# Pooled attention with an MLP: last keys scored over all rows, queries of two pairs transposed together, heads alternating in a batch's last pairs

## The chip, the cores and the metric

One core of a Trainium2 chip runs the whole program. The metric is device time in microseconds (us) of one execution. The kernel before takes 897.01 us, the median of three executions (896.06 to 898.55).

Engines as the profile names them: PE is the matrix engine, PEld its weight load, DVE the vector engine, ACT the scalar engine, POOL the GpSimd engine, SP the engine whose queue issues nearly all DMAs here.

## The reference

Four batches of eight heads, 1152 positions of 64 elements. Queries are averaged in twos, so 576 query rows stand against 1152 keys. The result, with the heads side by side (512 wide), goes through a layer norm and an MLP of width 2048 with a residual.

```python
def attn(q, k, v):                                    # (4, 8, 1152, 64) each
    q_pool = q.reshape(B, H, S // 2, 2, D).mean(axis=3)
    scores = np.matmul(q_pool, k.transpose(0, 1, 3, 2)) / np.sqrt(D)
    attn = np.exp(scores - np.max(scores, axis=-1, keepdims=True))
    attn = attn / (np.sum(attn, axis=-1, keepdims=True) + 1e-09)
    return np.matmul(attn, v)

x = attn_out.transpose(0, 2, 1, 3).reshape(B, S // 2, H * D)
xn = (x - mu) / np.sqrt(var + 1e-06) * g_ln
out = x + np.maximum(xn @ w_ch1, 0.0) @ w_ch2         # 512 -> 2048 -> 512
```

## The kernel before

**Tiling.** Heads are taken in pairs: 4 pairs a batch, 16 pairs in all, numbered p. A pair is nine steps, so there are 144 steps, numbered i with `p, j = divmod(i, 9)`. A step scores 128 query rows against all 1152 keys. Steps j = 0 to 3 are the first head, j = 4 is the last 64 rows of both heads, j = 5 to 8 the second head. Nearly every product is made with numbers split into a high and a low fp16 half, three matmuls for one (high by high, high by low, low by high).

**Scores** (`emit_s`, L320 to L344). The contraction is 64 long, and keys of even chunks lie on partitions 0 to 63, of odd chunks on 64 to 127. So the matmuls over 512 keys go in couples, one on the upper and one on the lower 64 rows of the array. The ninth chunk, the last 128 keys, has no partner: it takes three more matmuls of 128 columns on rows 0 to 63. A step has nine score matmuls (18 of half the width at j = 4).

**A step** (`step`, L924 to L986) is written out by hand. In program order a step i takes the row maximum of its scores (L350, DVE), issues the scores of step i + 1 (L337, PE), then for i the exponential (L364) and its high half (L378, both ACT). Then come the low half of step i - 1 (L387 on DVE; for j = 2, 5, 8 L244 and L385 on POOL), its DMA transpose through SP (L390), the product with V of step i - 4 (L433, 27 matmuls), one transposition for the next pair (`a_prep`) and one unit of the MLP (`some_units`). The first batch (steps 0 to 35, `on_pe`) is different: it transposes in fp32 on PE (L397, L421), has no MLP units, and DVE, ACT and POOL prepare the MLP's weights beside it.

**Next pair.** While a pair runs, k, v and q of the next come in through SP. The q tile holds two pairs, one on each half of the partitions, and has two buffers; its four loads stand together at step i0 - 2 of an even pair (i0 is the first step of the pair before it). POOL adds neighbouring queries (`pool_q`, L162) and copies the sum beside itself (`dup_q`, L168), ACT takes a bound of each tensor (`bound`, L180). Then `prep_k` and `prep_q` transpose on PE into a PSUM bank, and ACT and DVE split that into two fp16 halves. `PREPS` lists six for a pair: keys of each head, the last keys, and three units of six query chunks of 64 rows by 128.

**MLP units.** A 128-row tile t of a batch is normed (`norm`, `ln_a`, `ln_r`, `ln_t`) when all eight heads of it are there. Two normed tiles release `half_of` units into a queue: for each half w of the width four units of the first layer (L569, 24 matmuls) and four of the second (L600, 12 matmuls). The 64-row leftovers of two batches make a smaller set, `("h", g)`. A step takes one unit from the queue; after step 148 two. A batch of four tiles has 32 units. With the heads in order, tiles t = 0 to 3 of a batch become whole in the last pair's steps j = 5, 6, 7 and 8.

```python
key = ("h", b // 2) if j == 4 else (b, j if j < 4 else j - 5)
whole[key] = whole.get(key, 0) + 1
if whole[key] == 8 and key != ("h", 0):
    norms.append(key)
```

## Time and profile before

| what | value |
|---|---|
| median of three executions | 897.01 us |
| the profiled execution's own time | 892.43 us |
| its span from first to last instruction | 890.6 us |
| PE, DVE, ACT, POOL busy | 837.2, 611.8, 568.4, 346.6 us |
| granted PE clock, mean | 0.98 |

The busy time of PE is modelled from starts and sizes, and matmuls overlap in it, so a price is better read from the start of one group to the start of the next. The span runs from the first to the last instruction; the time of an execution is a little more.

### The profile page before, as it was taken

The numbers are of one execution on the slowest core, as the hardware profiler recorded it, in microseconds if no ns is written. First come the engines' busy times: TensorE is split into PE (matmuls) and PEld (weight loads), VectorE is DVE, ScalarE is ACT, GpSimd is POOL, SyncE is SP. The second block draws the span as 40 slices with busy tenths as digits, with TensorE's granted clock in tenths as the row PEclk, the third lists the DMA queues.
The fourth block names the chain that finished last, engine by engine and source line by source line (L and its number), as shares of the span: only waits on it lengthen the run. The fifth ranks groups of instructions, "written<-read, shape, count | busy, mean of one in ns | idle before, by whom it ended". The sixth has DMA issues, their size and how long they took to land.

```text
span 890.6 us, 22107 instructions
## 1 busy us (share of the span) xinstructions
PE 837.2 (94%) x9430; PEld 608.2 (68%) x9430; DVE 611.8 (69%) x1094; ACT 568.4 (64%) x851; POOL 346.6 (39%) x316
## 2 busy tenths in 40 slices
PE   8898979899799999996999999998999999999997
PEld 6787768677566676754758576676667576776664
DVE  3586988888787777778777777787777777532211
ACT  4888788788677777776677777676767666211110
POOL 3010543543988844336435243535543422300000
PEclk9999999999899999997999999999999999999999
DMA  4554154403498779997896979895979778310001
GB/s 130 196 157 164 50 194 126 172 1 96 92 179 168 141 150 183 180 169 137 154 193 114 203 141 188 127 186 107 222 121 175 129 129 143 57 25 13 13 13 24
DMA packets 271667, 114.95 MB, mean 129 GB/s; under 512 B 254928, under 2 KB 254928, under 8 KB 271568
## 3 DMA queue, kind: packets, MB, share of 16 engines
q1 hardware_dynamic: 271216, 112.65, 61.4%
q8 instruction: 74, 1.21, 0.6%
q10 hardware_dynamic: 352, 0.88, 0.4%
q14 instruction: 25, 0.20, 0.1%
HBM read 45.09 MB, written 4.72 MB: 56 GB/s over the span
## 4 chain that ended last, share of the span: by engine, by line
PE 54%; DVE 25%; ACT 10%; DMA 5%; issue 3%; POOL 2%; SPq 1%; ACTq 0%; POOLq 0%; DVEq 0%
PE psum L569 15%; PE psum L600 15%; DVE mx L350 7%; PE psum L337 7%; PE psum L433 7%; DVE hl L387 4%; PE psum L421 4%; DVE stage L107 3%; ACT pe L364 3%; PE psum L397 2%; DVE ht L583 2%; DVE wsl L107 2%; DVE kt L270 2%; DMA qr<-in_q_dram 2%; DMA kr<-in_k_dram 1%
## 5 line engine op out<-in xcount | busy, mean ns | idle before, releaser
L350 DVE TENSOR_REDUCE mx<-psum 128x1 f32<-128x1152 f32 x144 | 194.2, 1349 | 27.1 <-PE psum L433 18.9
L364 ACT ACTIVATE pe<-psum,nb,sc 128x1152 f32<-128x1152 f32 x144 | 188.9, 1312 | 32.0 <-DVE nb L355 23.6
L600 PE MATMUL psum<-wsl,ht 128*128 128x512 f16 x864 | 196.0, 379 | 0.2 <-DVE ht L583 0.2
L569 PEld LDWEIGHTS <-wsl 128*128 128x128 f16 x1920 | 170.9, 98 | 22.7 <-issue 2.7
L569 PE MATMUL psum<-xn,wsl 128*128 128x256 f16 x1536 | 177.3, 274 | 1.9 <-DVE xn L539 1.0
L337 PE MATMUL psum<-kt,qt 64*128 64x512 f16 (+3 forms) x1440 | 151.8, 332 | 24.7 <-ACT xb L488 13.9
L337 PEld LDWEIGHTS <-qt 64*128 64x128 f16 (+1 forms) x1440 | 70.9, 98 | 116.0 <-issue 66.4
L600 PEld LDWEIGHTS <-ht 128*128 128x128 f16 x864 | 81.8, 98 | 90.0 <-issue 0.4
L378 ACT ACTIVATE hl<-pe 128x1152 f16<-128x1152 f32 x108 | 125.7, 1163 | 5.0 <-DMA pt<-hl 1.6
L433 PE MATMUL psum<-vt,pt 128*128 128x65 f16 (+1 forms) x3240 | 119.8, 195 | 0.0
L433 PEld LDWEIGHTS <-pt 128*128 128x128 f16 (+1 forms) x3240 | 108.1, 101 | 9.4 <-issue 0.6
L488 ACT ACTIVATE xb<-psum,r 128x64 f32<-128x64 f32 x128 | 39.7, 311 | 109.4 <-DVE r L484 100.1
L244 POOL TENSOR_SCALAR pe<-pe 128x1152 f32<-128x1152 f32 x36 | 41.9, 1164 | 164.0 <-ACT hl L378 153.7
L387 DVE SCALAR_TENSOR_TENSOR hl<-pe,hl 128x1152 f16<-128x1152 f32 x72 | 104.3, 1448 | 0.0
L582 ACT ACTIVATE ht<-psum 128x512 f16<-128x512 f32 x72 | 42.7, 594 | 90.6 <-PE psum L569 90.2
L583 DVE SCALAR_TENSOR_TENSOR ht<-psum,ht 128x512 f16<-128x512 f32 x72 | 49.6, 690 | 66.2 <-ACT ht L582 65.4
L385 POOL TENSOR_TENSOR hl<-pe,hl 128x1152 f16<-128x1152 f32 x36 | 86.4, 2400 | 3.0
L421 PE MATMUL psum<-pt,vt 128*65 128x128 f32 (+1 forms) x720 | 81.6, 271 | 0.0
L421 PEld LDWEIGHTS psum<-pt,vt 128*65 128x65 f32 x720 | 75.8, 144 | 0.2 <-issue 0.2
L270 DVE SCALAR_TENSOR_TENSOR qt<-psum,s,qt 128x384 f16<-128x384 f32 x48 | 29.6, 616 | 46.9 <-ACT qt L273 46.9
L270 DVE SCALAR_TENSOR_TENSOR kt<-psum,s,kt 128x512 f16<-128x512 f32 (+1 forms) x48 | 31.5, 658 | 39.1 <-ACT kt L273 39.1
L403 ACT COPY pt<-psum 128x512 f32<-128x512 f32 x72 | 44.9, 639 | 10.8 <-PE psum L397 5.5
(112 smaller groups left out, 925.6 us busy)
## 6 DMA issues: line engine op xcount, KB each, us to landing
stage<-in_moe_w_ch_dram SPq DMA_DIRECT2D x32, 512.0 KB, 5.5
kr<-in_k_dram SPq DMA_DIRECT2D x16, 576.0 KB, 4.7
qr<-in_q_dram SPq DMA_DIRECT2D x31, 288.0 KB, 6.2
vr<-in_v_dram SPq DMA_DIRECT2D x15, 576.0 KB, 4.9
out_dram<-xb SPq DMA_DIRECT2D x32, 128.0 KB, 2.4
pt<-hl SPq DMA_TRANSPOSE x108, 5.0
vr<-in_v_dram ACTq DMA_DIRECT2D x1, 576.0 KB, 6.5
out_dram<-xh SPq DMA_DIRECT2D x4, 128.0 KB, 3.5
```

What stands on the lines that cost most here:

```text
L270: nc.vector.scalar_tensor_tensor(lo, ps, s, hi, op0=ALU.mult, op1=ALU.subtract)
L337: nc.tensor.matmul(out=sp[o:o + w, c0:c0 + n], lhsT=qt[r:r + 64, qa, q0:q0 + w], rhs=kt[r:r + 64, ka, h, k0:k0 + n], start=(a == 0), stop= ...
L350: nc.vector.tensor_reduce(mx, st["s"], axis=AX.X, op=ALU.max)
L364: nc.scalar.activation(out=st["pe"], in_=st["s"], func=ACTF.Exp, scale=pair[i // C]["sc"][:, 0:1], bias=st["nb"],)
L378: nc.scalar.activation(out=hl[:, 0], in_=st["pe"], func=ACTF.Copy, scale=2.0 ** 15)
L385: nc.gpsimd.tensor_tensor(hl[:, 1], st["pe"], hl[:, 0], op=ALU.subtract)
L387: nc.vector.scalar_tensor_tensor(hl[:, 1], st["pe"], 2.0 ** 15, hl[:, 0], op0=ALU.mult, op1=ALU.subtract)
L421: nc.tensor.matmul(out=ps[0:65, q0:q0 + w], lhsT=vt[:, h, c], rhs=pt[:, 128 * u + q0:128 * u + q0 + w], start=(u == 0), stop=(u == C - 1),)
L433: nc.tensor.matmul(out=dst[:, 0:n], lhsT=lhsT, rhs=rhs, start=(u == 0 and lhsT is hi and n == 65), stop=(u == C - 1 and lhsT is lo), skip_ ...
L569: nc.tensor.matmul(out=ps[:, o:o + n], lhsT=wsl[:, 8 * w + cc, wa, f * 128:f * 128 + 128], rhs=xn[:, xa * KD + cc, 0:n], start=(m == 0), s ...
L583: lambda: nc.vector.scalar_tensor_tensor(lo, pv, 0.0, hi, op0=ALU.max, op1=ALU.subtract),
L600: nc.tensor.matmul(out=ps, lhsT=hv[0][:, ha, f, t * 128:t * 128 + 128], rhs=wsl[:, 8 * w + 4 + f // 2, wa, (f % 2) * DM:(f % 2) * DM + DM] ...
```

## The change

The first part concerns the score matmuls. `load` brings the last chunk of keys a second time beside itself (one more DMA a pair, 64 KB), `prep_k` transposes both copies at once, so that the last 128 keys lie on all 128 partitions, the high half on 0 to 63 and the low half on 64 to 127 (tile `k8`). The three 128-column matmuls on 64 rows become two on 128 rows.

The second concerns the queries. From pair 6 (`JOINT`) on, one transposition takes a chunk of both pairs of a q tile (128 rows by 128), and writes its two halves 256 columns apart in the bank. There are five such units for two pairs, all while the pair before the even one runs, and the odd pair has only its three key units. The fp16 queries of two pairs share a tile (`qts`). The raw q tile has one buffer (`qraw`): before pair 6 each pair's half is loaded, pooled, copied and bounded by itself.

The third is the order of a batch's steps. `PLACES` gives head and tile of each step; in a batch's last two pairs the heads alternate, so tiles become whole at j = 1, 3, 6 and 8. In batch 0 the second layer's units of every second tile are cut into three of eight matmuls instead of two of twelve (`fine`), so that it has 36 units.

The fourth is the places of loads and helpers: k at i0 - 2 or i0 - 3, v at i0 - 1, q of the even pair at i0 - 6 and of the odd one at i0 - 5, `pool_q` and `dup_q` at i0 - 3 (before: i0 + 1), all preps that are due in a step at once.

```diff
+    JOINT = HP + 2
...
+    PLACES = [[(h, t) for h in range(2) for t in range(4)], [(h, t) for t in range(4) for h in range(2)]]
+    for x in PLACES:
+        x.insert(C // 2, None)
...
+        if which == "k":
+            r = raw_p.tile([128, 2, C + 1, D], FP32, tag="kr", name="kr")
+            eng.dma_start(out=r[:, :, 0:C], in_=x)
+            eng.dma_start(out=r[:, :, C], in_=x[:, :, C - 1])
...
         for h in range(2):
-            nc.tensor.transpose(ps[0:64, 128 * h:128 * h + 128], kr[:, h, C - 1], ident)
-        x = ps[0:64, 0:256].rearrange("p (h n) -> p h n", h=2)
-        return split_from((p, "k", 2), x, s[0:64, 0:1], kt[0:64, 0, :, 512:640], kt[0:64, 1, :, 512:640])
+            x = kr[:, h, C - 1:C + 1].rearrange("p c d -> p (c d)")
+            nc.tensor.transpose(ps[:, 128 * h:128 * h + 128], x, ident)
...
+        ms = range(4 * u, min(4 * u + 4, 2 * C))
+        x = ps.rearrange("p (v n) -> p v n", v=2)
+        for m in ms:
+            nc.tensor.transpose(x[:, :, 64 * (m % 4):64 * (m % 4) + 64], qr[:, chunk(m)], ident)
...
+    def preps_of(p):
+        if p < JOINT:
+            return PREPS
+        if p % 2:
+            return [x for x in PREPS if x[0] is prep_k]
+        x = PREPS + ((prep_q, 3), (prep_q, 4))
+        return x if p != HP else x[:3] + (x[4], x[3]) + x[5:]
...
-        wide = ((64, 0, 512, 0), (0, 512, 512, 0))
-        for here in (wide, ((0, 1024, 128, 512),)):
-            for a, r, c0, n, k0 in [(a, *x) for a in range(3) for x in here]:
...
+        for a in range(3):
+            ka, qa = ((0, 0), (1, 0), (0, 1))[a]
+            for r, c0 in ((64, 0), (0, 512)):
+                for h, c, w, o in parts:
                     nc.tensor.matmul(
...
+        for qa in range(2):
+            for h, c, w, o in parts:
+                nc.tensor.matmul(
+                    out=sp[o:o + w, 1024:1152],
+                    lhsT=qt[:, qa, c:c + w], rhs=pair[p]["k8"][:, h],
+                    start=(qa == 0), stop=(qa == 1),
+                )
...
         units.extend(
-            (2 * w + 1, 2 + f0 // 2, lambda t=t, f0=f0: l2(t, f0))
-            for t in range(len(xs)) for f0 in (0, 4)
+            (2 * w + 1, (m1 + 5) // 6, lambda t=t, m0=m0, m1=m1: l2(t, m0, m1))
+            for t in range(len(xs))
+            for m0, m1 in (((0, 8), (8, 16), (16, 24)) if t and fine else ((0, 12), (12, 24)))
         )
...
+        elif p < JOINT:
+            half = (64 * (p % 2), 64)
+            at(i0 - 2, load_q, p, (nc.sync,))
+            pre(i0 + 1, other_half, p)
+            pre(i0 + 1, pool_q, p, nc.gpsimd, (half,))
+            at(i0 + 1, dup_q, p, nc.gpsimd, (half,))
+            at(i0 + 2, bound, p, "q", *half)
+        elif p % 2 == 0:
+            at(i0 - 6, load_q, p, (nc.sync,))
+            at(i0 - 5 if ahead else i0 - 1, load_q, p + 1, (nc.sync,))
+            iq = i0 - 3 if ahead else i0 + 1
+            pre(iq, pool_q, p, nc.gpsimd)
+            at(iq, dup_q, p, nc.gpsimd)
+            at(iq + 1, bound, p, "q")
...
-        key = ("h", b // 2) if j == 4 else (b, j if j < 4 else j - 5)
+        key = ("h", b // 2) if j == 4 else (b, PLACES[p % HP // 2][j][1])
...
-            a_prep()
+            for _ in range(max(len(preps), 1)):
+                a_prep()
```

## Rows read from the trace of the kernel before

**Rows 1.** The profile page: busy time, and the chain's shares by engine.

```profile
PE 837.2 (94%) x9430; PEld 608.2 (68%) x9430; DVE 611.8 (69%) x1094; ACT 568.4 (64%) x851; POOL 346.6 (39%) x316
...
PE 54%; DVE 25%; ACT 10%; DMA 5%; issue 3%; POOL 2%; SPq 1%; ACTq 0%; POOLq 0%; DVEq 0%
```

**Rows 2.** Windows by stage: stretch and its length, busy us and instructions by engine, clock, DMA.

```profile
14.30:203.90 189.60, 168.95 (x1676) 142.01 (x1677) 153.03 (x246) 152.62 (x281) 62.10 (x47) 0.97 0.38 124
203.90:232.00 28.10, 20.95 (x209) 16.23 (x209) 24.23 (x50) 20.38 (x32) 16.11 (x22) 0.92 0.36 87
232.00:266.60 34.60, 33.56 (x391) 24.19 (x390) 24.58 (x41) 24.45 (x34) 31.99 (x24) 0.92 0.86 165
398.40:429.30 30.90, 23.10 (x281) 16.32 (x280) 23.82 (x50) 21.43 (x29) 20.37 (x28) 0.78 0.83 153
429.30:591.50 162.20, 159.96 (x2001) 110.40 (x2001) 124.75 (x225) 117.22 (x157) 64.49 (x59) 1.00 0.87 165
591.50:621.00 29.50, 27.00 (x398) 20.40 (x397) 22.45 (x46) 18.74 (x25) 17.14 (x20) 1.00 0.57 106
```

**Rows 3.** The same windows for L350 alone, one row maximum a step: DVE busy.

```profile
203.90:232.00 28.10, 8.03 (x6) 0.92 0.36 87
...
398.40:429.30 30.90, 6.68 (x5) 0.78 0.83 153
429.30:591.50 162.20, 44.54 (x33) 1.00 0.87 165
591.50:621.00 29.50, 6.71 (x5) 1.00 0.57 106
```

**Rows 4.** Timeline of PE at two batch ends; in brackets idle time and releaser.

```profile
404.98 1.81 PE L337 MATMUL psum<-kt,qt 64*64 64x512 f16 x18 [2.82 <-ACT pe L364]
...
419.81 0.63 PE L287 MATMUL psum<-ident,kr 128*64 128x128 f32 x2 [3.92 <-DVE kt L270]
...
603.57 0.63 PE L532 MATMUL psum<-ident,xs 128*128 128x128 f32 x4 [1.70 <-DVE kt L270]
```

**Rows 5.** Timeline of PE, a step without a prep: start us, us, what.

```profile
728.87 0.99 PE L337 MATMUL psum<-kt,qt 64*128 64x512 f16 x9
729.79 0.99 PE L433 MATMUL psum<-vt,pt 128*128 128x65 f16 x27
730.62 2.78 PE L569 MATMUL psum<-xn,wsl 128*128 128x256 f16 x24
733.33 1.01 PE L337 MATMUL psum<-kt,qt 64*64 64x512 f16 x18
```

**Rows 6.** Timeline of PE in the tail, first-layer units of 128 columns.

```profile
791.90 5.52 PE L569 MATMUL psum<-xh,wsl 128*128 128x128 f16 x96
797.26 5.34 PE L600 MATMUL psum<-wsl,ht 128*128 128x512 f16 x24
```

**Rows 7.** Timeline of PE, transpositions of keys (L284) and of queries (L298).

```profile
529.14 0.66 PE L284 MATMUL psum<-ident,kr 128*128 128x128 f32 x4
529.63 2.75 PE L600 MATMUL psum<-wsl,ht 128*128 128x512 f16 x12
...
533.24 0.99 PE L433 MATMUL psum<-vt,pt 128*128 128x65 f16 x27
534.16 0.59 PE L298 MATMUL psum<-ident,qr 64*128 64x64 f32 x6
534.68 0.82 PE L600 MATMUL psum<-wsl,ht 128*128 128x512 f16 x3
```

**Rows 8.** The q tile's instructions: duration ns, lowest, median and highest.

```profile
L180 ACT ACTIVATE qt<-qr x9: 1146/1152/1163, 7.7 to 640.7; 128x1152 f16<-128x1152 f32 x7, 64x1152 f16<-64x1152 f32 x2
...
L162 POOL TENSOR_TENSOR qr<-qr x8: 2613/2622/2624, 13.1 to 631.2; 128x1152 f32<-128x1152 f32 x7, 64x1152 f32<-64x1152 f32 x1
...
DMA to landing us min/median/max: 4.0/6.2/9.3
```

**Rows 9.** Timeline of POOL, the low half of a step on it.

```profile
561.27 2.37 POOL L385 TENSOR_TENSOR hl<-pe,hl 128x1152 f16<-128x1152 f32 x1
```

More of the change, by code (lines that the diff above doesn't have):

```diff
@@ L95, in tile_pooled_attention_moe @@
     raws = {}
+    qraw = raw_p.tile([128, 2, C, 2, D], FP32, name="qraw")
     fill, soon = deque(), deque()
@@ L291, in prep_q, with low @@
+        def low():
+            nc.vector.scalar_tensor_tensor(
+                k8[64:128], x[64:128], s[64:128, 0:1], k8[64:128], op0=ALU.mult, op1=ALU.subtract
+            )
+            have.add((p, "k", 2))
+        return (lambda: nc.scalar.activation(out=k8, in_=x, func=ACTF.Copy, scale=s[:, 0:1]), low)
     def prep_q(p, u):
         o = 64 * (p % 2)
-        qr = raws[p, "q"][o:o + 64].rearrange("p h c r d -> p (h c) (r d)")
+        qr = raws[p, "q"].rearrange("p h c r d -> p (h c) (r d)")
@@ new lines, in prep_q @@
+        if p < JOINT:
+            for m in range(6):
+                nc.tensor.transpose(
+                    ps[:, 64 * m:64 * m + 64], qr[o:o + 64, chunk(6 * u + m)],
+                    ident[o:o + 64, o:o + 64],
+                )
+            c = slice(384 * u, 384 * u + 384)
+            hi, lo = (qt[:, a, p % 2, c] for a in range(2))
+            return split_from((p, "q", u), ps[:, 0:384], s[:, 1:2], hi, lo)
+        ms = range(4 * u, min(4 * u + 4, 2 * C))
+        x = ps.rearrange("p (v n) -> p v n", v=2)
@@ L597, in l2 @@
             ps = acc[t]
-            for f in range(f0, f0 + 4):
-                for ha, wa in ((0, 0), (0, 1), (1, 0)):
-                    nc.tensor.matmul(
-                        out=ps,
-                        lhsT=hv[0][:, ha, f, t * 128:t * 128 + 128],
-                        rhs=wsl[:, 8 * w + 4 + f // 2, wa, (f % 2) * DM:(f % 2) * DM + DM],
-                        start=(f == 0 and ha == 0 and wa == 0),
-                        stop=(f == 7 and ha == 1),
-                    )
-            if f0 == 0:
+            for m in range(m0, m1):
+                f = m // 3
+                ha, wa = ((0, 0), (0, 1), (1, 0))[m % 3]
+                nc.tensor.matmul(
+                    out=ps,
+                    lhsT=hv[0][:, ha, f, t * 128:t * 128 + 128],
+                    rhs=wsl[:, 8 * w + 4 + f // 2, wa, (f % 2) * DM:(f % 2) * DM + DM],
+                    start=(m == 0), stop=(m == 23),
+                )
+            if m1 < 24:
                 return ()
@@ L772, in behind_scales, with other_half @@
         nc.gpsimd.memset(state(1)["acc"][0:64, 1:2], 0.0)
+    def other_half(p):
+        o = 64 - 64 * (p % 2)
+        nc.gpsimd.memset(state(p)["acc"][o:o + 64, 1:2], 0.0)
     for p in range(1, NP):
         i0 = (p - 1) * C
-        at(max(i0 - 1, 0), load, p, "k", nc.sync)
-        at(i0, load, p, "v", nc.sync)
-        at(i0 + 1, bound, p, "k")
-        if p % 2 == 0:
-            at(i0 - 2, load_q, p, (nc.sync,))
-            pre(i0 + 1, pool_q, p, nc.gpsimd)
-            at(i0 + 1, dup_q, p, nc.gpsimd)
-            at(i0 + 2, bound, p, "q")
-        elif p == 1:
+        old, late = p <= HP + 1, 1 if on_pe(i0) else 0
+        ahead = 1 if p > JOINT else 0
+        if old:
+            lk = max(i0 - 1, 0)
+        else:
+            lk = i0 - 2 if p % 2 or not ahead else i0 - 3
+        at(lk, load, p, "k", nc.sync)
+        at(i0 - ahead, load, p, "v", nc.sync)
+        at(i0 + 1 if old else i0, bound, p, "k")
+        if p == 1:
             upper = (64, 64)
@@ L827, in half @@
                 w, keep["xn", u], [xb[b][:, u], xb[b][:, u + 1]],
-                [[(64 * s, rows(b, 2 * x + s)) for s in range(2)] for x in (u, u + 1)],
+                [[(64 * s, rows(b, 2 * x + s)) for s in range(2)] for x in (u, u + 1)], b == 0,
             )
```

127 lines of the change are left out of this document (65 added, 62 removed).

## The prediction

> **What bounds it now.** I read the page first, then windows by stage, then PE's timeline inside a step, and last what PE waits for. PE is busy 94% of the span and holds over half of the chain of waits; DVE holds a quarter of it [rows 1]. The windows split this into stages [rows 2]. In 429.3 to 591.5 PE is busy 159.96 of 162.20 us. These are 33 steps [rows 3], 4.92 us each, in which DVE works 124.75 / 33 = 3.78 us and ACT 3.55. PE sets the pace there, and PE work taken away is time taken away, until a step comes near 3.8 us. The first batch, 14.3 to 203.9, is different: 36 steps of 5.27 us, PE busy 168.95, DVE 153.03, ACT 152.62. No engine is full; each waits for another in turn. Two short stretches are different again. In 203.9 to 232.0, six steps, PE is busy 20.95 of 28.10 us. In 398.4 to 429.3, five steps, it is busy 23.10 of 30.90, and the granted clock is 0.78 instead of 1.00, so part of this stretch ran at 1.2 GHz after PE had stood still.
>
> The queue of MLP units explains the second stretch. Batch 0 has 32 units, one a step, from step 41 to 72. Batch 1 releases its first ones at step 77 (tiles 0 and 1 become whole at j = 5 and 6 of its last pair, four steps go by until their product with V, then norm and transposition), so steps 73 to 77 have none. PE then waits for the exponential and for the evacuation of banks [rows 4]; DVE meanwhile does four norms in four steps. From batch 1 on there are 40 units, more than steps, so later borders have work; the border of batch 2 is 591.5 to 621.0, five steps with five units in 29.50 us [rows 2, 3].
>
> **The score matmuls.** In a step without a prep the nine score matmuls run from 728.87 to 729.79, 0.92 us, the 27 with V 0.83, the unit 2.71 [rows 5]. A stream of 128-column matmuls with a new weight each goes at (797.26 - 791.90) / 96 = 0.056 us [rows 6]. Three become two, both kernels leave the half-array mode once a step, so a step saves 0.056. Bounds: nothing, if the new two cost more than the old each, and 0.11 if one also hides a weight load. At j = 4 the new ones are 64 columns wide on 128 rows, a mode between two others, and one more change of mode (below: 0.09) eats the gain. So 8 of 9 steps save 0.056: 96 steps of the PE-bound stage give 5.4 us; the first batch's 32 steps (1.8 us) I count under the first batch.
>
> **The queries.** Before a unit, 27 matmuls with V take 0.83 us [rows 5]; before query transpositions they take 0.92 [rows 7], so entering the 64-row mode costs 0.09. Six query transpositions with their exit take 0.52 (534.16 to 534.68). That is 0.61 a unit, and 3.66 for the six units of two pairs. Four 128-row transpositions take 0.49 (529.14 to 529.63), with no change of mode, so 18 take 2.2 [rows 7]. Pairs 6 to 15 are five couples: 5 x 1.46 = 7.3 us. Upper bound 7.9, with the first one's start taken out. Lower bound below zero: no row shows a transposition that writes two runs of a bank, and if each cost as much again (0.12 us), 90 of them give 11 back. I take the row as it stands, since a run of 64 words is not short.
>
> The Trainium skill, page PSUM — Partial Sum Buffer, section Specifications (TRN2), says that PSUM's lines are 8 bytes and that an access pattern that is not contiguous slows matmuls significantly. By it the 90 transpositions would gain nothing or lose; no run here shows such a write.
>
> The last keys' transposition goes from 64 to 128 columns of weights and its evacuation from 64 to 128 partitions, with the same elements in each partition: nothing.
>
> **Units that come earlier.** With heads alternating, tiles become whole at j = 1, 3, 6, 8. For batch 0 tile 1 is normed at step 34 instead of 37 and the first unit can run at step 38 instead of 41. For batch 1 the first unit comes at step 75 instead of 78. Batch 0 has 36 units, in steps 38 to 73. That leaves one step, 74, without a unit in place of five. The border of batch 1 with units should then cost no more than that of batch 2 does: 29.50 us against 30.90, and four units of 2.6 leave the tail. 1.4 + 10.4 = 11.8; I take 11. Bounds: 4, if each unit that comes in adds 1.9 us to its step, and 14.
>
> At the first border three units come in. The same six steps took 28.10 without and the next six 34.60 with six units [rows 2], so a unit adds 1.1 us and takes 2.6 out of the tail: 4.5, and I take 4 (0 to 6), since POOL's queue is as full there.
>
> The four additional units are the price. Twelve of eight matmuls stand for eight of twelve; only if those twelve steps really get 0.87 shorter is nothing lost. Such a step has 0.92 + 0.83 + 1.73 of PE and 0.3 of preps, 3.8 us, just DVE's own 3.78. I charge 3 of 10.4 us (0 to 7).
>
> Norms two or three steps apart, not four in a row, should also shorten waits at batch 2's border, of which the longest is 1.70 us [rows 4]: 1.5 (0 to 2.5).
>
> **Loads and helpers.** The second load of the last key chunk is 64 KB on SP's queue beside 576 KB that it issues anyway; the keys are asked for two to three steps ahead of their first transposition, which covers it. If that cover were gone, the transposition of the last keys would be late by the few us that a load takes to land, once a pair. SP's order is otherwise kept: each load stands at the end of the step that frees its tile, ahead of the next DMA transpose, which waits for DVE anyway.
>
> On POOL, `pool_q` (2.62 us [rows 8]) moves to j = 6, in front of the low half of step j = 5 (2.37 us for its subtraction [rows 9]). It waits for a load issued a step before, and POOL is in order. Behind it are the low half, whose fp32 tile the exponential two steps on needs again, and the DMA transpose. Four pairs (8, 10, 12, 14) meet this. I charge 1.5 us in all (0 to 8), because the exponential is itself ahead of PE in this stage.
>
> **The first batch.** 1.8 us of score matmuls go. Pairs 3 and 5 get a bound on ACT (1.15 us) and a `pool_q` (2.62 us, on 64 partitions as on 128 [rows 8]) of their own, since the odd half is no longer done with the even one. ACT is busy 0.80 of this stage. I count 0, plus or minus 2.
>
> **The sum.** 5.4 + 7.3 + 11 + 4 + 1.5 - 3 - 1.5 = 24.7 us. The profiled execution took 892.43 us (span 890.6 and 1.8 around it): 867.7. The median of the runs is 1.0051 of it, 897.01; the same factor gives 872 us.
>
> **Rivals.** *The refill gives little.* Units that come earlier land in steps that DVE and ACT pace, and the cut units lose their whole price. For it: DVE's 3.78 us a step [rows 2, 3]. Against: batch 2's border takes five units in less time than batch 1's five steps without. The border is then worth 4, the first one 0, the cut units cost 3: 13.7 us of gain, 883 us.
>
> *PE's savings are hidden.* If a shorter PE step only makes PE wait for the exponential, the 12.7 us of scores and queries go: 885 us. Against: steps of 4.46 us without a prep run back to back with nothing idle between [rows 5].
>
> *The strided transposition.* At double price the queries lose 3.7 in place of gaining 7.3: 883 us. It is what the rule of the Trainium skill, page PSUM — Partial Sum Buffer, section Specifications (TRN2), would do here.
>
> *Slower.* POOL's new order: if q lands late (up to 9.3 us after its issue [rows 8]) `pool_q` blocks POOL, the low half of j = 5 ends late, the exponential of j = 7 waits, then the scores. It decides from 24.7 / 4 = 6.2 us lost at each of the four places. A landing at 9.3 in place of 6.2, with the 2.62 of `pool_q` and the copy behind it, makes 7 to 8: 4 x 7.5 against the 1.5 counted gives about 901 us.
>
> **How the numbers follow.** The forecast has 0.59, its own range 860 to 880. The refill 0.18, the hidden savings 0.10, the strided write 0.07, POOL 0.06. The first four are faster by more than 0.3% (2.7 us, about what a measurement of this kernel can tell from no change; the three runs spread as much). A few hundredths of them may end near zero: faster 0.90, same 0.04, slower 0.06. The range from 858, where the border gives 14 and the cut units cost nothing, to 889, past the three faster rivals, holds about 0.8.
>
> **What would show it.** Score matmuls 1,280 in place of 1,440, query transpositions 198 in place of 288. The stretch near 400 us should have units in four of its five steps and a clock near 1.00; at 0.78 again, the refill failed. PE's wait for the exponential and for DVE's evacuations should lose its long entries [rows 4]. From one group of four joint transpositions to what follows should be 0.49 us; 0.9 would be the strided write. The low half on POOL should begin less than 3 us later at j = 5 of pairs 6, 8, 10 and 12; if the scores two steps on wait for the exponential there, that is the slower rival. I would be wrong most likely in the 11 us of batch 1's border or in the 3 us of the cut units.

## The result, and the profile after

The changed kernel takes 909.78 us, the median of four executions (908.96 to 913.53), against 897.51 for the kernel before beside it: ratio 1.0146, 95% interval 1.0114 to 1.0178. It is slower by 1.5%. The forecast was 872, and the time lies outside its range. The profiled execution took 909.41 us, its span is 907.4.

The page of the changed kernel, busy time and the chain's shares, answers to [rows 1].

```profile
PE 826.9 (91%) x9180; PEld 584.8 (64%) x9180; DVE 624.7 (69%) x1087; ACT 569.6 (63%) x850; POOL 361.6 (40%) x324
...
PE 40%; DVE 31%; ACT 16%; DMA 5%; issue 5%; POOL 2%; SPq 0%; ACTq 0%; POOLq 0%; DVEq 0%
```

PE works 10 us less and the span is 17 us longer (the medians differ by 12.3; the kernel before took 892.43 us when it was profiled): PE's share of the chain went from 54 to 40%, DVE's from 25 to 31, ACT's from 10 to 16. PE now waits. The windows by stage, with the columns of [rows 2], say where. They begin at the scores of steps 0, 36, 42, 72 and 81; the last is the tail behind the last scores.

```profile
14.20:200.90 186.70, 166.86 (x1644) 138.91 (x1644) 154.45 (x252) 154.41 (x285) 67.34 (x57) 0.96 0.41 128
200.90:231.80 30.90, 26.52 (x265) 20.35 (x264) 24.54 (x43) 23.03 (x35) 20.61 (x21) 1.00 0.56 121
231.80:267.00 35.20, 27.49 (x307) 16.15 (x307) 24.80 (x40) 19.50 (x28) 26.13 (x19) 0.95 0.60 119
398.60:452.20 53.60, 45.08 (x526) 30.53 (x525) 38.79 (x72) 34.78 (x47) 25.58 (x28) 0.94 0.76 154
452.20:596.00 143.80, 132.22 (x1584) 85.62 (x1583) 110.25 (x189) 96.28 (x130) 59.17 (x51) 1.00 0.81 153
775.46:907.00 131.54, 126.71 (x1106) 87.16 (x1105) 37.73 (x66) 22.65 (x39) 7.90 (x16) 1.00 0.15 32
```

The fifth row is the reading that matters: 27 steps behind batch 1's border, where PE had been full (159.96 of 162.20 us, [rows 2]), now leave it idle for 11.6 of 143.8 us. What PE waits for in the whole span is in the list of waits (what waits, for whom, us in total, times, longest):

```profile
PE psum L215 <- DVE dg L210: 11.5, 7, 2.6
PE psum L388 <- ACT xb L537: 10.5, 11, 1.9
PE psum L298 <- DVE kt L280: 9.4, 7, 2.8
PE psum L323 <- DVE kt L280: 8.5, 3, 4.2
PE psum L206 <- ACT kt L190: 5.1, 3, 3.9
```

The second row was there before (L337 waited 13.9 us for ACT's xb). The others have grown: in the kernel before these waits were 1.3, 3.9 (one wait), 0.8 and 2.8 us. L215 and L206 are the two matmuls by which a pair's maxima cross the partitions (`all_max`), L298 the last keys, L323 the query units of a single pair. In the 27 steps of the fifth row above L215 leads with 5.3 us.

For all that follows one table of stretches serves, taken from the starts of score groups in each kernel's profiled execution (us). Each stretch comes from one execution, the ratio from all of them; e1's and e11's profiled executions are 4.5 and 6.6 us longer than their medians. Where kernels share a stretch's program, S81 to S138 agrees within 1.1 us (0.2 among e2, e5, e8, e12 and e14). Up to S36 the changed kernel and the e kernels other than e7 have the same steps, and range from 200.9 to 204.6; the nine steps from S36 take 56.5 to 58.6 in four kernels that have the same steps there (changed, e1, e2, e5).

| kernel | to S36 | S36 to S81 | S81 to S138 | S138 to S143 | tail | ratio to before, 95% |
|---|---|---|---|---|---|---|
| before | 203.9 | 230.8 | 294.1 | 22.2 | 139.5 | 1 |
| changed | 200.9 | 251.4 | 301.1 | 22.1 | 131.9 | 1.0146, 1.0114 to 1.0178 |
| b1, last keys only | 204.6 | 231.4 | 294.6 | 22.1 | 139.5 | 0.9983, 0.9961 to 1.0006 |
| b2, alternating only | 202.2 | 235.9 | 294.8 | 22.3 | 131.4 | 0.9954, 0.9932 to 0.9977 |
| b3, alternating and cut | 203.9 | 236.4 | 294.7 | 22.3 | 131.4 | 0.9953, 0.9928 to 0.9978 |
| b4, last keys, alternating | 204.2 | 239.4 | 294.4 | 22.1 | 131.3 | 0.9934, 0.9913 to 0.9954 |
| e1, POOL behind | 202.6 | 247.3 | 300.9 | 22.1 | 132.0 | 1.0071, 1.0039 to 1.0103 |
| e15, diagonal on ACT | 202.8 | 249.0 | 295.7 | 22.1 | 131.9 | 1.0114, 1.0083 to 1.0144 |
| e11, both | 204.6 | 246.3 | 289.9 | 22.1 | 131.9 | 0.9951, 0.9924 to 0.9978 |
| e7, both, ACT everywhere | 206.1 | 245.3 | 290.1 | 22.1 | 132.2 | 1.0018, 0.9996 to 1.0040 |
| e5, scales back | 201.7 | 241.8 | 290.7 | 22.1 | 131.9 | 0.9921, 0.9898 to 0.9944 |
| e2, all helpers back | 202.1 | 243.1 | 290.8 | 22.1 | 132.0 | 0.9967, 0.9941 to 0.9993 |
| e3, no joint queries | 201.9 | 237.0 | 297.4 | 22.1 | 131.3 | 0.9969, 0.9948 to 0.9990 |
| e13, no joint, loads ahead | 202.2 | 242.5 | 298.2 | 22.1 | 131.3 | 1.0012, 0.9989 to 1.0035 |
| e16, no joint, late keys | 201.6 | 236.1 | 294.5 | 22.1 | 131.4 | 0.9932, 0.9908 to 0.9956 |
| e8, no doubled prep | 202.0 | 245.9 | 290.9 | 22.1 | 131.3 | 0.9971, 0.9952 to 0.9989 |
| e9, the same in the changed | 202.4 | 254.4 | 300.0 | 22.1 | 131.3 | 1.0154, 1.0122 to 1.0186 |
| e10, e8 with late keys | 203.0 | 246.0 | 293.0 | 22.1 | 131.4 | 1.0024, 1.0001 to 1.0046 |
| e12, keys last in pair 5 | 202.3 | 240.6 | 290.7 | 22.1 | 131.4 | 0.9877, 0.9844 to 0.9910 |
| e14, e12 not cut | 201.8 | 239.2 | 290.7 | 22.1 | 131.3 | 0.9912, 0.9882 to 0.9943 |

In these two executions the change wins 3.0 us up to step 36, which is no more than that spread, and 7.6 in the tail, and loses 20.6 from step 36 to 81 and 7.0 from 81 to 138.

### The profile page after: what moved, and what is told of

Same layout as the page of the kernel before. It is cut to its first block, busy times and chain, and to the rows that moved or that the text cites. A ratio compares the mean times of both kernels' runs of the same rounds, so it can differ in the third digit from the quotient of the medians.

```text
span 907.4 us, 21663 instructions
## 1 busy us (share of the span) xinstructions
PE 826.9 (91%) x9180; PEld 584.8 (64%) x9180; DVE 624.7 (69%) x1087; ACT 569.6 (63%) x850; POOL 361.6 (40%) x324
## 4 chain that ended last, share of the span: by engine, by line
PE 40%; DVE 31%; ACT 16%; DMA 5%; issue 5%; POOL 2%; SPq 0%; ACTq 0%; POOLq 0%; DVEq 0%
PE psum L650 12%; PE psum L618 10%; DVE mx L399 9%; DVE hl L436 6%; ACT pe L413 4%; PE psum L470 4%; PE psum L482 4%; DMA pt<-hl 3%; PE psum L380 3%; DVE ht L632 3%; PE psum L446 2%; DVE stage L111 2%; ACT ht L631 2%; ACT qt L283 2%; DVE dg L210 1%
## 5 line engine op out<-in xcount | busy, mean ns | idle before, releaser
L618 PE MATMUL psum<-xn,wsl 128*128 128x256 f16 x1536 | 180.3, 276 | 1.5 <-DVE ht L632 0.8
L380 PE MATMUL psum<-kt,qt 64*128 64x512 f16 (+1 forms) x960 | 121.8, 380 | 3.2 <-ACT pe L413 2.3
L482 PEld LDWEIGHTS <-pt 128*128 128x128 f16 (+1 forms) x3240 | 110.3, 101 | 2.3 <-issue 0.2
L436 DVE SCALAR_TENSOR_TENSOR hl<-pe,hl 128x1152 f16<-128x1152 f32 x72 | 108.8, 1512 | 3.5 <-ACT hl L427 3.5
L380 PEld LDWEIGHTS <-qt 64*128 64x128 f16 (+1 forms) x960 | 34.3, 96 | 55.7 <-issue 36.2
L388 PEld LDWEIGHTS <-qt 128*128 128x128 f16 (+1 forms) x320 | 17.9, 99 | 72.5 <-issue 72.0
L280 DVE SCALAR_TENSOR_TENSOR qt<-psum,s,qt 128x512 f16<-128x512 f32 (+2 forms) x43 | 28.5, 663 | 42.7 <-ACT qt L283 42.7
L388 PE MATMUL psum<-kt,qt 128*128 128x128 f16 (+1 forms) x320 | 41.4, 226 | 12.1 <-ACT xb L537 10.5
```

What stands on the lines that cost most here:

```text
L380: nc.tensor.matmul(out=sp[o:o + w, c0:c0 + 512], lhsT=qt[r:r + 64, qa, c:c + w], rhs=kt[r:r + 64, ka, h], start=(a == 0), stop=(a == 2),)
L436: nc.vector.scalar_tensor_tensor(hl[:, 1], st["pe"], 2.0 ** 15, hl[:, 0], op0=ALU.mult, op1=ALU.subtract)
L482: nc.tensor.matmul(out=dst[:, 0:n], lhsT=lhsT, rhs=rhs, start=(u == 0 and lhsT is hi and n == 65), stop=(u == C - 1 and lhsT is lo), skip_ ...
L618: nc.tensor.matmul(out=ps[:, o:o + n], lhsT=wsl[:, 8 * w + cc, wa, f * 128:f * 128 + 128], rhs=xn[:, xa * KD + cc, 0:n], start=(m == 0), s ...
```

## Experiments: POOL's order and the early scales

Two theories at first. *POOL*: the rival of the prediction, the query sums in front of the low half of j = 5. *Scales*: what the prediction had not priced, the maxima's reduction (`scales_reduce`) and the bound of v one step earlier from pair 7 on, and the bound of q four steps earlier for the even pairs from 8 on. A third, *joint queries*, blamed the eight units that gather in every second pair.

The timeline of POOL in the changed kernel shows the first theory at step 59 (pair 6, j = 5): start us, us, what; in brackets idle time and releaser. Its high half was written by 336.94 (first row, ACT); the next rows are POOL's, the last two the exponential of step 61 on ACT and the scores of step 63 on PE.

```profile
335.78 1.16 ACT L427 ACTIVATE hl<-pe 128x1152 f16<-128x1152 f32 x1
...
340.46 2.62 POOL L171 TENSOR_TENSOR qraw<-qraw 128x1152 f32<-128x1152 f32 x1 [10.44 <-DMA qraw<-in_q_dram]
343.05 1.15 POOL L254 TENSOR_SCALAR pe<-pe 128x1152 f32<-128x1152 f32 x1
344.29 3.38 POOL L434 TENSOR_TENSOR hl<-pe,hl 128x1152 f16<-128x1152 f32 x1
...
347.70 1.31 ACT L413 ACTIVATE pe<-psum,nb,sc 128x1152 f32<-128x1152 f32 x1 [4.31 <-POOL hl L434]
...
349.06 0.82 PE L380 MATMUL psum<-kt,qt 64*128 64x512 f16 x6 [1.32 <-ACT pe L413]
```

POOL stands idle until the odd half's load lands, sums, and only then takes up the low half, 6.1 us after it could have; at the other three places it is 10.3, 5.4 and 5.1 us. The load itself is not slow. The four DMAs of the q tile, the odd half's two among them, land within 5.7 us of their issue, and the median of [rows 8] is 6.2:

```profile
DMA to landing us min/median/max: 4.0/4.9/5.7
```

The exponential of step 61 starts 0.03 us behind the low half's end, and the scores of step 63 wait 1.32 us for it. At two of the other places the exponential starts as close behind the low half, but there, and at the fourth, no wait of PE in the next 11 us is longer than 0.6 us. The DMA transposes, in order on SP, are late as well. In the waits of SP's queue, the changed kernel first and then e5, the transpose stands for POOL:

```profile
SPq L439 <- POOL vr L254: 43.6, 8, 8.8
```

```profile
SPq L439 <- POOL vr L254: 18.6, 7, 4.0
```

**e1** moves the sums one step, behind that low half.

```diff
-            iq = i0 - 3 if ahead else i0 + 1
+            iq = i0 - 2 if ahead else i0 + 1
```

> The changed kernel, with the sums of neighbouring queries on POOL one step later, so that they stand behind the low half of step j = 5 and no longer in front of it (four pairs: 8, 10, 12, 14). Theory POOL: this order alone makes the low half, the DMA transposes behind it and the exponentials late; the four places lose about 5 us each in the trace, so the time falls by some 20 us, from 910 to about 890. Theory scales: what PE waits for is the chain of bounds and scales that now runs a step earlier on ACT and DVE; the time falls by less than 4 us, to 906 to 910. Theory joint queries: the preps that gather in every second pair are the cause; again 906 to 910.

902.39 us, ratio 1.0071: 6.7 us come back, not 20 (the span of the profiled execution is 2.5 us shorter). POOL's order is real and is not the whole.

**e2** sets the helpers of pairs 7 to 15 to the places that pair 6 has (the keys' load and bound stay a step early).

```diff
-        ahead = 1 if p > JOINT else 0
+        ahead = 0
```

> The changed kernel with the helpers of pairs 8 to 15 at the places that pair 7 has: query sums on POOL at j = 1, bounds, scales and the load of v a step later. Joint transpositions and alternating heads stay. Theory POOL: as with the query sums alone moved back, about 890. Theory scales: PE loses its waits for the diagonal of maxima (about 11 us in the trace) and for the bound of v (about 5.6 us), so about 893 here, and more than 10 us below the run that only moves the query sums. Theory joint queries: 904 to 910, since the preps stay where they are.

891.94 us, 0.9967: 9.3 us more than e1. The scales are in it. The timeline of the changed kernel at step 84 (DVE, then POOL, then PE) shows what they wait for:

```profile
471.05 0.27 DVE L209 TENSOR_REDUCE mx<-psum 3x1 f32<-3x128 f32 x1
471.35 2.38 DVE L210 TENSOR_SCALAR dg<-ident,mx 3x3 f32<-3x3 f32 x1
...
471.36 2.36 POOL L434 TENSOR_TENSOR hl<-pe,hl 128x1152 f16<-128x1152 f32 x1
...
472.22 0.30 PE L388 MATMUL psum<-kt,qt 128*64 128x128 f16 x4
473.79 0.38 PE L215 MATMUL psum<-dg,ones 3*128 3x3 f32 x2 [1.27 <-DVE dg L210]
```

The diagonal of the maxima is a 3 x 3 operation, 0.22 us long alone. Here it starts with POOL's subtraction, within 0.01 us, and ends 0.02 behind it, at 473.74. From pair 7 on it takes 2.21 to 2.38 us in four pairs and 1.74 in a fifth, ending 0.02 us behind a subtraction of POOL each time, and 0.22 to 0.24 in the four others. A step earlier means j = 3, and that is just where POOL has the low half of j = 2. In the kernel before it fell on j = 4, where POOL has no low half, and took 0.22 to 0.25 from pair 7 on. Its durations in ns in the whole run (lowest, median, highest), before and changed; the 1046 is pair 5's, beside POOL's work on the MLP's weights:

```profile
L200 DVE TENSOR_SCALAR dg<-ident,mx x20: 201/216/1046, 11.1 to 691.5; 3x3 f32<-3x3 f32 x13, 1x1 f32<-1x1 f32 x4, 2x2 f32<-2x2 f32 x3
```

```profile
L210 DVE TENSOR_SCALAR dg<-ident,mx x20: 201/217/2385, 11.0 to 713.5; 3x3 f32<-3x3 f32 x13, 1x1 f32<-1x1 f32 x4, 2x2 f32<-2x2 f32 x3
```

**e7** gives the diagonal to ACT, on top of e1; **e11** does so from step 36 on (its edit beside e1's is below); **e15** does the same without e1's edit.

```diff
-                nc.vector.tensor_scalar(dg[0:n, 0:n], ident[0:n, 0:n], mx[0:n], None, op0=ALU.mult)
+                if not this or on_pe(this[0]):
+                    nc.vector.tensor_scalar(dg[0:n, 0:n], ident[0:n, 0:n], mx[0:n], None, op0=ALU.mult)
+                else:
+                    nc.scalar.activation(out=dg[0:n, 0:n], in_=ident[0:n, 0:n], func=ACTF.Copy, scale=mx[0:n])
```

> The changed kernel with the query sums behind the low half of j = 5, and besides with the 3 x 3 diagonal of the maxima made by ACT and no longer by DVE; everything else stays a step early. In the trace this operation, 0.22 us long alone, takes up to 2.38 us on DVE and ends 0.02 us behind a subtraction of POOL, in five or six pairs, and PE waits for it 10.5 us in all. Theory DVE behind POOL: on ACT it does not wait, PE loses these waits, and the time falls by 7 to 10 us against the run that only moves the query sums (ratio to before near 0.998). Theory scales early in general (ACT's bounds and DVE's queue late, whatever this operation takes): no more than 3 us (ratio 1.004 to 1.008).

896.17 us, 1.0018: 4.7 us, below the 7 to 10 expected. The stretches hint why: 10.8 us less from 81 to 138, but 3.5 more up to step 36, where it was on DVE without such waits. That 3.5 is no more than the spread of this stretch; e11 is the test of it.

> The changed kernel with the query sums behind the low half of j = 5, and the diagonal of the maxima on ACT from step 36 on, on DVE in the first batch. With it on ACT everywhere the ratio was 1.0018; that trace lost some 3.5 us in the first batch and won some 11 behind step 81. Theory DVE behind POOL: the whole 10.5 us of waits go, ratio 0.995 to 0.998. If the loss in the first batch was chance: 1.001 to 1.003.

890.29 us, 0.9951: 10.7 us below e1, as the first theory said, and 6 below e7, from which it differs in the first batch alone. In e11's groups PE's wait for the diagonal is 3.5 us in place of 11.5 (the last figures: idle time before the group):

```profile
L218 PE MATMUL psum<-dg,ones 3*128 3x3 f32 (+2 forms) x40 | 8.0, 267 | 3.5 <-ACT dg L213 2.8 <-DVE dg L211 0.7
```

> The changed kernel with only the diagonal of the maxima on ACT from step 36 on; the query sums stay in front of the low half of j = 5. If POOL's order and the diagonal's wait cost independently (6.7 and 10.7 us): ratio 1.002 to 1.004. If the late low half keeps the exponentials late whatever the maxima do, so that the gain is swallowed: 1.008 or more. If POOL's order hurts only through the diagonal: 0.994 to 0.998.

903.91 us, 1.0114: alone it gives 2.9 us, and the two intervals overlap. With the diagonal free, POOL's order costs 14.6 us (e15 to e11); with POOL's order mended, the diagonal costs 10.7; together they are 17.5. So either one left in place hides part of what the other's repair is worth. The spans of the profiled executions (907.4, e1 904.9, e15 901.4, e11 894.8) have the same sign but other sizes: the diagonal 6.0 alone and 10.1 behind e1, POOL's order 2.5 and 6.6. Which of the two costs more is not settled.

**e5** keeps the early loads and sets sums, bounds of q and v, and scales back.

```diff
-            iq = i0 - 3 if ahead else i0 + 1
+            iq = i0 + 1
...
-            at(i0 + 2 - ahead, bound, p, "v")
-        pre(i0 + 3 - ahead, scales_reduce, p, 0, 2 if on_pe(p * C) else 3)
+            at(i0 + 2, bound, p, "v")
+        pre(i0 + 3, scales_reduce, p, 0, 2 if on_pe(p * C) else 3)
```

> The changed kernel with query sums, bounds of q and v and the scales back at pair 7's places, but the loads of k, v and q as early as the change puts them. Theory scales: as without any early helper, ratio 0.995 to 0.998. Theory loads: if early loads on SP's queue, in front of the DMA transposes, were part of the loss, 1.001 to 1.005.

890.16 us, 0.9921. The early loads are no part of the loss here; by the ratios they win 4 us against e2 (1.8 by the spans), though the intervals just touch. What the early bounds and the early sums cost beside the diagonal is e11 to e5, 2.7 us, which is within both intervals.

## Experiments: scores, heads and units

**b1** is the kernel before with the score part alone (as in the change, in `load`, `kt_of`, `prep_k` and `emit_s`).

```diff
-        wide = ((64, 0, 512, 0), (0, 512, 512, 0))
-        for here in (wide, ((0, 1024, 128, 512),)):
...
+        for qa in range(2):
+            for h, q0, w, o in parts:
+                nc.tensor.matmul(
+                    out=sp[o:o + w, 1024:1152],
+                    lhsT=qt[:, qa, q0:q0 + w], rhs=pair[p]["k8"][:, h],
```

> The kernel before with the last keys on all rows and nothing else. By the term of my sum: 0.056 us in eight of nine steps, 5.4 us and up to 1.8 in the first batch: ratio 0.992 to 0.994. By the groups in the traces since (0.921 to 0.875 us in plain steps, but 0.939 to 1.04 at j = 4 and 0.919 to 0.968 in front of the maxima): some 0.2 us a pair, 2 to 3 us in all, ratio 0.997 to 1.000.

892.82 us, 0.9983, not to be told from nothing or from 3 us. Its timeline of PE, a plain step and then j = 4:

```profile
730.64 0.82 PE L351 MATMUL psum<-kt,qt 64*128 64x512 f16 x6
731.40 0.29 PE L358 MATMUL psum<-kt,qt 128*128 128x128 f16 x2
731.52 0.98 PE L452 MATMUL psum<-vt,pt 128*128 128x65 f16 x27
...
735.05 0.84 PE L351 MATMUL psum<-kt,qt 64*64 64x512 f16 x12
735.82 0.30 PE L358 MATMUL psum<-kt,qt 128*64 128x128 f16 x4
736.06 0.99 PE L452 MATMUL psum<-vt,pt 128*128 128x65 f16 x27
```

The plain group is 0.88 us from first start to the product with V, against 0.92 in [rows 5] (medians between S81 and S108, in b4 and before: 0.875 and 0.921): 0.046 and not 0.056. At j = 4 it is 1.01; the timeline of the kernel before has 734.27 - 733.33 = 0.94 there. Over 57 steps the stretch S81 to S138 is 294.6 against 294.1: no gain shows.

```profile
734.27 0.99 PE L433 MATMUL psum<-vt,pt 128*128 128x65 f16 x27
```

**b2** is the kernel before with `PLACES` alone (the queries in the order of the steps and the second head's keys before the second query unit, as in the change), **b3** has the cut units as well, **b4** is b2 with b1's part.

```diff
-        key = ("h", b // 2) if j == 4 else (b, j if j < 4 else j - 5)
+        key = ("h", b // 2) if j == 4 else (b, PLACES[p % HP // 2][j][1])
```

> The kernel before with the alternating heads and nothing else (units not cut). Three units come in at the first border and three steps at the second only shift. By my sum 4 for the first border and 1.5 for the spread norms: ratio 0.994. If a unit that comes in early costs what it saves in the tail: 1.000. If the run with both (0.9934) has its gain from here and not from the scores: 0.993.

> The kernel before with the alternating heads and the second layer's units of batch 0 cut in 36, so that the queue is empty for one step in place of five. By my sum 11 + 4 + 1.5 - 3 = 13.5 us: ratio 0.985. If the steps of the border are paced by other engines and the refill is given back: as without the cut, 0.994 to 1.000, or slower by the 3 us of the cut units.

> The kernel before with only the last keys on all rows and the alternating heads (no joint queries, loads and helpers as before, MLP units not cut). By the terms of my sum: 5 for the scores, 15 for the two borders, 1.5 for the spread norms: about 876. If units that come earlier only land in steps that other engines pace (theory refill given back): 890 to 895. If alternation itself costs (norms and units beside full DVE steps): 897 or slower.

b2 takes 889.18 us (0.9954), b3 890.19 (0.9953), b4 889.83 (0.9934). The heads' order gives 4 us, the cut none that shows. The windows of the tail, behind the last scores, show it, for the kernel before, b2 and b3 in turn (columns of [rows 2]):

```profile
751.10:890.60 139.50, 134.78 (x1179) 94.20 (x1178) 41.84 (x73) 23.23 (x40) 7.97 (x17) 1.00 0.15 29
```

```profile
755.14:886.50 131.36, 126.72 (x1107) 87.21 (x1106) 37.72 (x66) 22.49 (x39) 7.80 (x15) 0.99 0.17 32
```

```profile
757.35:888.70 131.35, 126.72 (x1107) 87.20 (x1106) 37.73 (x66) 22.49 (x39) 7.81 (x15) 0.99 0.17 32
```

The tail is shorter by 8.1 us, three units, with the cut and without. 36 units for 32 fill four more steps, but with the same work.

## Experiments: joint queries

**e3** is the changed kernel without joint queries, and so without early helpers and without pair 5's doubled prep (below); its keys are still loaded at i0 - 2 from pair 6 on. **e13** is e5 without joint queries, **e16** is e3 with keys loaded at i0 - 1 and bounded at i0 + 1, as before.

```diff
-    JOINT = HP + 2
+    JOINT = NP + 2
...
-            lk = i0 - 2 if p % 2 or not ahead else i0 - 3
+        lk = max(i0 - 1, 0)
...
-        at(i0 + 1 if old else i0, bound, p, "k")
+        at(i0 + 1, bound, p, "k")
```

> The changed kernel with each pair's queries transposed by themselves in all 16 pairs (three units of six transpositions), which also puts the query sums on POOL at j = 1 of every pair and the helpers at their later places. Theory joint queries: the eight preps in one pair are the cause, so the time falls below the run that keeps them with the same places of helpers, by 10 us or more, to about 890. Theories POOL and scales: the places of the helpers are the cause and joint transpositions themselves save 7 us as forecast, so this is about 7 us slower than the run that keeps them.

> The run with early loads and the scales back (0.9921), with each pair's queries transposed by themselves. Theory transition: joint transpositions save 0.73 us a pair from pair 8 on, as the traces show from step 84 to 141 (4.7 us), and the first couple gives 6 us back; both runs are then equal within 0.2%. If joint queries save nothing anywhere: also equal, but without the difference of slope from step 84 on. If they cost: this is faster, 0.988.

> The run without joint queries (0.9969), with the keys' load and bound a step later as in the kernel before. Against the kernel before with last keys and alternating heads (0.9934) it still has the single raw q tile (each pair's half loaded, summed and bounded by itself), the preps of a step at once and the cut units. If the single q tile costs some 3 us: 0.996 to 0.999. If the early keys were the cost: 0.993 to 0.995.

892.32 us (0.9969), 897.35 (1.0012) and 888.78 (0.9932). The first two did not tell what they were meant to. A pair that transposes six units has its last key unit at i0 - 2 of the next pair; in e13 the keys of half the pairs are loaded before that, and wait in SP's queue for it, with the DMA transposes behind them. In the waits of SP's queue, e13 first and then e16, the load of keys stands 10 us longer, four times more. In e3 it doesn't (48.6 us); why its keys at i0 - 2 cost 2.9 us from S81 to S138 stays open.

```profile
SPq L123 <- PE psum L294: 58.7, 9, 29.2
```

```profile
SPq L123 <- PE psum L294: 48.6, 5, 29.2
```

So e16 is the kernel to compare with. It is b4 with the single raw q tile, the cut units and a step's preps all at once, and these together cost nothing that shows (0.9932 against 0.9934). From S81 to S138 e16 takes 294.5 us and the kernels with joint queries and late scales 290.7 to 290.9 (but for e10): 3.8 us for three couples. But e16 loads its keys at i0 - 1 and those at i0 - 2 or i0 - 3, and the keys' place matters to both kinds. With the same place in both it is 6.6 us (e3 to e2, keys at i0 - 2) or 1.5 (e16 to e10, keys at i0 - 1). From S36 to S81 the joint kernels lose 4.5 (e12) or 5.7 (e5). One reason is in the changed kernel's timeline of PE, between the scores of steps 44 and 45:

```profile
247.77 0.63 PE L294 MATMUL psum<-ident,kr 128*128 128x128 f32 x4
252.58 0.90 PE L323 MATMUL psum<-ident,qraw 64*128 64x64 f32 x6 [4.18 <-DVE kt L280]
253.41 4.01 PE L650 MATMUL psum<-wsl,ht 128*128 128x512 f16 x12
257.35 0.82 PE L380 MATMUL psum<-kt,qt 64*128 64x512 f16 x6
```

So that the single raw q tile is free for pair 7's half in time, pair 5 has two preps in one step. The second prep waits 4.18 us for the split of the first one's bank (by the program, since a unit of the second layer holds the other free one), and the unit behind takes 4.01 us in place of 2.75.

**e8** (from e2) and **e9** (from the changed kernel) undo the doubling, load pair 7's half a step later and sum the halves of pairs 6 and 7 by themselves, one a step. **e10** is e8 with late keys. **e12** (from e5) puts pair 5's second keys last instead and loads pair 6's keys later. **e14** is e12 without the cut.

```diff
-            if p == JOINT - 1 and n > 3:
-                n -= 1
...
-            at(i0 - 5 if ahead else i0 - 1, load_q, p + 1, (nc.sync,))
+            at(i0 - 5 if ahead else i0 if p == JOINT else i0 - 1, load_q, p + 1, (nc.sync,))
```

> The run with the helpers of pair 7 for all later pairs (ratio 0.9967), and besides pair 5's two last query units one step later each, so that no step has two preps that do not belong to the joint units (the odd half of the next couple is then loaded a step later and its sum made a step later). In the trace the doubled step, 44 to 45, takes 11 us, with 3.97 us of PE waiting for the split of the keys' bank and a unit that takes 4.35 in place of 2.75 us behind that wait. Theory doubled prep: this one step costs 5 to 6 us, so the ratio is 0.990 to 0.991, and the joint queries' 7 us are real. Theory joint queries give nothing: another wait takes its place, ratio 0.995 to 0.998.

> The changed kernel with the same undoing of the doubled prep in pair 5 and nothing else. Theory doubled prep: 5 to 6 us below the changed kernel's 1.0146, so 1.008 to 1.009. If later waits (POOL's order, scales early) swallow it: 1.012 to 1.015.

> The run without the doubled prep, with the keys' load and bound besides a step later, at the places of the kernel before, in all pairs. If the early load of keys in late pairs is worth nothing: same as that run. If SP's queue or ACT's order at i0 costs: up to 3 us faster (0.003).

893.89 us (0.9971), 912.25 (1.0154), 897.76 (1.0024): nothing won. In e8's timelines of ACT and PE a wait for ACT's bound takes the doubled prep's place. The bound of the queries waits 3.40 us for POOL's second sum, the bound of v stands behind it on ACT, and PE needs both:

```profile
276.93 1.16 ACT L190 ACTIVATE qt<-qraw 128x1152 f16<-128x1152 f32 x1 [3.40 <-POOL qraw L171]
278.09 1.15 ACT L190 ACTIVATE kt<-vr 128x1152 f16<-128x1152 f32 x1
...
279.38 0.38 PE L206 MATMUL psum<-ident,acc 128*3 128x128 f32 x1 [4.15 <-ACT kt L190]
```

My own edit put a wait in the place of the one removed. Early keys do pay here: e10 is 0.5% behind e8.

The edit of e12, beside the first two lines above:

```diff
+        if p == JOINT - 1:
+            return PREPS[:3] + PREPS[4:] + PREPS[3:4]
...
-            lk = i0 - 2 if p % 2 or not ahead else i0 - 3
+            lk = i0 if p == JOINT else i0 - 2 if p % 2 or not ahead else i0 - 3
```

> The run with early loads and the scales back (0.9921), with pair 5's preps in another order: its three query units one a step and the second head's keys last, so that no step has two of them and the odd half of the next couple is loaded as early as before; the keys of pair 6 are loaded two steps later. In the run that delayed the query half, a wait of 4.22 us for the bound of the queries took the place of the doubled prep. Theory doubled prep: 5 to 6 us, ratio 0.985 to 0.987. If pair 6's later keys make ACT's bound late in the same way, or other waits swallow it: 0.990 to 0.994.

> The run with the keys last, and the MLP units of batch 0 not cut (32, five steps without a unit). My sum had 11 - 3 us for the refill: this would be 0.9% slower than the run with the cut. By the accounts since, the cut moves no work out of the tail, since it only makes four more units of the same work: equal within 0.2%.

e12 takes 886.43 us, 0.9877, the lowest of all: 1.2% below the kernel before and 0.4% below e5, less than the 5 to 6 us expected, though its interval still overlaps that of e5. The gain is in the right place: its trace loses 6.8 us less than e5's from S36 to S45, of which 2.9 are left at S51. e14 takes 888.52 us, 0.9912; its interval overlaps that of e12.

The joint units themselves, in e12's timeline of PE:

```profile
490.10 0.66 PE L333 MATMUL psum<-ident,qraw 128*128 128x128 f32 x4
490.59 2.75 PE L652 MATMUL psum<-wsl,ht 128*128 128x512 f16 x12
```

## Why the prediction was wrong

By the runs, the ratio goes from 1 to 0.9932 (e16: last keys, alternating heads, cut units, single q tile), 0.9921 (e5: joint queries and early loads), 0.9951 (e11: bounds and scales a step early) and 1.0146 (diagonal on DVE, sums in front). With 896 us that is -6.1, -1.0, +2.7 and +17.5.

**Loads and helpers: the step that failed.** The forecast charged 1.5 us for POOL's new order, on the ground that the exponential is itself ahead of PE, and nothing for the rest. Measured are 20.2 us for both (e5 to the changed kernel). The ground does not hold at step 59: the exponential waits 4.31 us for the low half there, and the scores wait 1.32 us for the exponential. And the forecast followed the loads and `pool_q` and left out that the same part of the change moves the bounds and the reduction of the maxima to earlier steps. That brought in a cost that is neither named nor bounded: a 0.22 us operation of DVE that lands beside POOL's subtraction and ends with it. By the ratios POOL's order costs 6.7 us with the diagonal in place and 14.6 without, the diagonal 2.9 and 10.7; the rest, 2.7, is not clear of the noise.

The slower rival named the right place: the sum blocks POOL, and the low half begins 5.1 to 10.3 us late at all four places, where the sign of being wrong was 3. It had 0.06. But its condition, a load that lands late, was not needed, since landings of 5.7 us and less sufficed. Its price of 7.5 us a place was too high (14.6 / 4 = 3.7 at most), and its last step, scores that wait for the exponential, is seen at one place of four, so where most of the cost arises stays open. That the time came near the rival's 901 is partly luck: it is owed to two causes, of which the rival had one.

**The refill of batch 1's border: wrong.** 11 us stood for four units that leave the tail. The cut that fills the four steps makes four more units of the same work, so nothing leaves it: 131.4 us with and without. I had charged the cut units as a price (3 us) without seeing that they are the refill. Of 13.5 us for both borders, norms and cut, 4.2 are there (b3). What was sound in it is the first border, with 4 us forecast. In b2 three units leave the tail, which is 8.1 us shorter, and S36 to S81, which holds both borders, is 5.1 longer, so 3.0 are left in the traces and 4.1 by the ratio. With all 36 units the granted clock from step 72 to 81 is 0.94 in the changed kernel, where it was 0.86 in the kernel before, so less of it ran at 1.2 GHz. PE waits there all the same, busy for 45.08 of 53.60 us in the changed kernel, and the nine steps get no shorter by the cut (49.5 us in b2, 49.9 in b3). The kernel before, from step 72 to 81:

```profile
387.40:434.70 47.30, 39.23 (x480) 27.11 (x479) 36.24 (x70) 31.61 (x41) 23.89 (x30) 0.86 0.77 142
```

**The scores: mis-sized.** 5.4 us forecast, 1.5 by b1's ratio and none in the PE-bound stretch. The rate of 0.056 comes from a tail row and is 0.046 in place; the change of mode at j = 4, named as a bound, costs 0.07, and a smaller one comes up in front of the maxima (0.92 to 0.97). By these a pair should still win 0.2 us; that the stretch shows none is not settled.

**The queries: price of a unit right, net wrong.** 1.46 us a couple were forecast. Behind step 81, where three couples (10 and 11, 12 and 13, 14 and 15) are transposed, 3.8 / 3 = 1.27 are measured against e16, but 0.5 or 2.2 where both kernels load their keys at the same place. That 1.27 comes near the forecast is therefore no proof of it. Four transpositions take 0.49 us in place, as forecast. The strided write is thus no rival any more: the Trainium skill, page PSUM — Partial Sum Buffer, section Specifications (TRN2), says that patterns that are not contiguous slow matmuls significantly, and with runs of 64 words no such price shows. But between steps 36 and 81, where the first two couples are, the joint kernels lose more than they win behind it; the two preps in one step are one reason. By the ratios e5 is 1.0 us better than e16, which is within the noise, and e12 4.9.

The first batch (0, plus or minus 2) is not contradicted: it takes 200.9 to 204.6 us in the fourteen kernels that have its changed steps, 203.9 before, and no cost of the single q tile shows.

The gap between 872 and 909.78 is 37.8 us. By the ratios it is 18.7 for the helpers, 9.3 for borders and cut, 6.3 for the queries, 3.9 for the scores: 38.2. By the intervals each of these is uncertain by some 3 us, so the good sum says little about the single terms.

Open: where PE pays for POOL's order beside step 59; why S81 to S138 does not show the scores' 0.2 us a pair; how the keys' place and the joint queries act on each other; why the joint kernels still lose 4.5 us from S36 to S81 with the doubled prep gone; and whether the cut is worth the 0.35% between e12 and e14.

## What to carry to other kernels

When a change moves a step, list every instruction that it issues, the small ones on every engine too, and look what runs on the other engines at the new place: here a 3 x 3 operation cost 10.7 us once POOL's order was mended. Work that is cut into more pieces fills more slots and moves nothing; count what leaves the tail in work, not in units. Repair two suspected waits separately and together: each repair alone showed 2.9 and 6.7 us of 17.5.

## What the runs showed of the hardware

A DVE operation of 0.22 us took up to 2.38 us when it met a POOL subtraction, and ended with it; on ACT it took 0.28 to 0.30 us (e11). The Trainium skill, page SBUF — State Buffer, section Who interferes with whom, says that DVE and GpSimd share one pair of ports under an exclusive lock, that whoever issues first holds it for the whole instruction while the other is blocked, that `tensor_scalar` can run in a mode that needs the pair, and that a DVE operation with two inputs in SBUF contends with GpSimd's reads. The trace agrees in that the diagonal ends 0.02 us behind POOL's operation each time. The lock itself is not in a trace, and with starts 0.01 us apart the trace does not tell who was first. It goes the other way, too: POOL's subtraction at 344.29 took 3.38 in place of 2.37 us, having started behind a low half of DVE, which runs from 344.09 to 345.43:

```profile
344.09 1.35 DVE L436 SCALAR_TENSOR_TENSOR hl<-pe,hl 128x1152 f16<-128x1152 f32 x1
```

And a wait on PE can be paid twice: behind the 4.18 us of the doubled prep the granted clock is 0.68 over the next unit, so part of it ran at 1.2 GHz, and its twelve matmuls take 4.01 us in place of 2.75. By the window from there to the next scores:

```profile
253.41:257.35 3.94, 3.94 (x13) 1.40 (x13) 2.10 (x3) 1.63 (x2) 0.00 (x0) 0.68 0.94 225
```
